# Packed products for four batches in two row tiles, and the first batch through DRAM, in an attention and mixture-of-experts kernel

## The chip, the core and the metric

The kernel runs as one program on one core of a Trainium2 chip. The metric is the device time of one execution in microseconds; the median of three runs of the kernel before is 1287.91 us (1282.92 to 1290.34). A core has TensorE (PE in the profile, its weight loads PEld), VectorE (DVE), ScalarE (ACT), GpSimd (POOL) and SyncE (SP). Each engine works through its own queue in order. Here SP issues nearly all DMAs.

## The reference, cut to what matters

```python
def sm_attn(qq, kk, vv):                       # softmax(scale * qq kk^T) vv
    ...
p_packed = sm_attn(p, k, v)                    # p: 8 batches, 8 heads, 32 rows of 64; k, v: 576 rows
x = sm_attn(q, p_packed, p_packed)             # q: 576 rows; every head attends to 32 packed rows
x = x.transpose(0, 2, 1, 3).reshape(4608, 512)
h = np.maximum(x @ w_in, 0.0)                  # w_in 512 x 2048
x2 = (h * h) @ w_out                           # w_out 2048 x 512
logits = x2 @ w_gate + modality_bias[modality_id]
e = np.argmax(logits, axis=1)                  # one of 8 experts for each token
out[token] = gate[token] * (np.maximum(x2 @ w1[e], 0.0) @ w2[e])
```

The weights w_in and w_out come as 64-bit floats.

## The kernel before

The program has an attention part, a layer part and an expert part. In the expert part, and in the layer part from its second unit on, nothing is changed by hand.

**The trick of the first layer.** `softmax(...) @ p_packed @ w_in` is computed as `softmax(...) @ (p_packed @ w_in)`. The inner product is small: each batch and head has 32 packed rows, and with w_in they give a 256 x 2048 matrix a batch, called pw. The first layer is then a product of the second softmax (256 wide) with pw. To keep precision, each factor stands as two tiles, a high half (rounded to float32r by an ACT copy) and a low half (the difference), and a product is three matmuls: high by low, high by high, low by high.

**Attention (lines 283 to 348, and the loop at 888).** The work is cut into 16 quads: a batch and four of its heads. `att1` is a generator of four steps: score products L297 (two column tiles of 64), then maximum, exp (L310) and a scaling of the whole 128x576 tile (L315), then five transposes (L320, L321) and their copies (L322, L323), then the value products L329 and L330 and the copies of the packed rows into `pp32` (L334) and into `pphl`, the two halves (L346 on ACT, L347 on POOL). The loop starts a quad in each round and takes one step of each quad that is under way, so a quad ends three rounds after it starts. A round also takes two conversions of w_in (`convert`, lines 198 to 216: ACT, four DVE operations, ACT, POOL), from 64 bits to the two halves in `wbt`.

**The packed product (`pw_unit`, lines 352 to 378).** `pphl` holds a pair of batches and a pair of heads as a block-diagonal 128x128 tile. A unit is one pair of heads and 512 of the 2048 columns; for each of the four pairs of batches it takes three matmuls L361 of 128x128 by 128x512, one PSUM bank and one copy out. Pairs 1 to 3 go to the DRAM tile `pw_d`. Of pair 0, batch 0's half is split at once into the two halves of its blocks (L376 on ACT, L377 on POOL), and batch 1's half goes to `pw_d`. A batch read back from `pw_d` (`load_pw`, two DMAs for 512 columns, into one of two buffers called raw) is split in 16 blocks by `split_pw` (L404 on ACT, L405 on POOL). The blocks live in a ring of 18, `head` (8) and `ring` (10).

**Layers (the loop at 959).** The 4608 tokens are 12 units of 384. For each unit and each of 16 blocks f, `layer1` multiplies (L473), ACT makes relu, square and high half (L482 to L484), the low half follows (L486: POOL in the first unit, DVE later), and `layer2` (L493) adds to three PSUM banks. `layer2` needs w_out in `wbt`, and w_out is converted into the very slots that w_in leaves: conversion u of w_out waits for all packed products of unit u. `others(u)`, called ahead of the first unit and in it, emits what is left of the packed products and one conversion of w_out.

**What sets the order.** The kernel is written in one order; a scheduler in the build then gives each engine its own, from a timeline that it works out itself. So a `yield` or a call count moves the emission, and only through the scheduler the place in a queue.

Of the kernel before, what the change touches and what calls it, by code (L numbers as in the profile page):

```python
# [26 lines left out]
def tile_pack_attention_moe_moe2(  # L27
# [33 lines left out]
    PAIRS = B // 2  # L61
    UPP = NUN // PAIRS
# [34 lines left out]
    pphl = pw_p.tile([P, PAIRS, 2, HP, 2 * P // 2], F32R, name="pphl")  # L97
# [42 lines left out]
    pw_d = tc.dram_tile([PAIRS, HP, P, DFF], F32, name="pw_d")  # L140
# [80 lines left out]
    PW = {9 + i: [(0, 2 * i), (0, 2 * i + 1)] for i in range(4)}  # L221
    PW |= {13 + i: [(1, 2 * i), (1, 2 * i + 1)] for i in range(6)}
    for i in range(3):
        PW[16 + i].append((2, i))
    A20 = 4
# [57 lines left out]
    def att1(i):  # L283
# [23 lines left out]
        sm = a_p.tile([P, 1], F32, tag="sm", name="sm")  # L307
# [7 lines left out]
        nc.scalar.activation(out=a, in_=a, func=AF.Copy, scale=sm)  # L315
# [8 lines left out]
        yield  # L324
        pq = bank("t", "pq")
        for g in range(2):
            ds, ns = slice(2 * g * D, 2 * (g + 1) * D), slice(2 * g * NPK, 2 * (g + 1) * NPK)
            for r in range(4):
                nc.tensor.matmul(pq[:, ns], vt[:, r, ds], aT[:, r, ns], start=(r == 0), stop=False)  # L329
            nc.tensor.matmul(pq[:, ns], vl[:, ds], aT[:LAST, 4, ns], start=False, stop=True)  # L330
        load_v(i + 4)
        gs = slice(2 * qd, 2 * qd + 2)
        for j in range(2):
            nc.vector.tensor_copy(  # L334
                pp32[j * D : (j + 1) * D, b, gs, j * NPK : (j + 1) * NPK],
                pq[j * D : (j + 1) * D, :P].rearrange("p (g i n) -> p g i n", g=2, i=2)[:, :, j, :],
            )
        hl = pphl[:, b // 2].rearrange("p x g (b n) -> p x g b n", b=2)
        if b < 2:
            places = [(slice(2 * qd + i, 2 * qd + i + 1), (b + i) % 2) for i in range(2)]  # L340
        else:
            places = [(gs, b % 2)]
        for g, o in places:
            src = pp32[:, b, g, :]
            hi = hl[:, 0, g, o, :]
            nc.scalar.activation(out=hi, in_=src, func=AF.Copy)  # L346
            nc.gpsimd.tensor_tensor(out=hl[:, 1, g, o, :], in0=src, in1=hi.bitcast(F32), op=ALU.subtract)  # L347
# [4 lines left out]
    def pw_unit(bp, u, so=None):  # L352
        if (bp, u) in made:
            return
        made.add((bp, u))
        fb, hp = divmod(u, HP)
        w = wbt[:, u]
        hl = pphl[:, bp]
        ph = bank("t", "pw")
        for i, (x, y) in enumerate(((0, 1), (0, 0), (1, 0))):  # L360
            nc.tensor.matmul(ph, hl[:, x, hp], w[:, y, :], start=(i == 0), stop=(i == 2))  # L361
        if so is None:
            so = pw_p.tile([P, 512], F32, tag="w5", name="pws", bufs=3)
        if bp % 2:
            nc.vector.tensor_copy(so, ph)
        else:
            nc.scalar.activation(out=so, in_=ph, func=AF.Copy)
        cs = slice(fb * 512, (fb + 1) * 512)
        if bp:
            nc.sync.dma_start(pw_d[bp, hp, :, cs], so)  # L370
        else:
            lo = slice((hp % 2) * 64, (hp % 2) * 64 + 64)
            up = slice(64 - (hp % 2) * 64, 128 - (hp % 2) * 64)
            t = blocks(4 * fb, 4)[lo, :, :, hp // 2, :]
            pv = so[lo].rearrange("p (k f) -> p k f", k=4)
            nc.scalar.activation(out=t[:, :, 0, :], in_=pv, func=AF.Copy)  # L376
# [511 lines left out]
    for i in range(len(quads) + 3):  # L888
# [5 lines left out]
        if i >= 3:  # L894
            runs.pop(0)
# [18 lines left out]
    def others(u):  # L914
        for v in range(min(u + HP + 1, NU)):
            pw_unit(0, v)
# [144 lines left out]
```

## Time and profile before

| | |
|---|---|
| median of three runs | 1287.91 us |
| profiled execution | 1283.14 us, span 1281.3 us |
| mean granted TensorE clock | 0.977 of full |
| PE busy | 1234.5 us (96%) |
| PE weight loads | 1029.2 us (80%) |
| DVE, ACT, POOL busy | 810.7, 600.7, 323.9 us |
| last score product L297 ends | 108.8 us |
| first layer-2 matmul L493 starts | 143.2 us |

A busy time is an interval that the engine's instructions cover. A matmul's interval begins where it enters the array and includes its way through, so those of neighbours overlap: the time that one costs in a stream is the distance between starts, not its own length. A float32 matmul shows as two, a float32r matmul as one. In a row, `128*64` is the part of the array that a matmul uses, rows by columns. What stands in brackets at a row's end is the idle time of the engine before it and what ended that.

### The profile page before, as it was taken

The page shows a single profiled execution, that of the slowest core. Times are in us where ns is not written, and L with a number is a line of the kernel's source. Part 1 is how long each engine was busy: PE and PEld are TensorE (multiplying, and loading weights), DVE is VectorE, ACT ScalarE, POOL GpSimd, SP SyncE. Part 2 cuts the span into 40 slices and gives each one's busy share as a digit, 9 for nine tenths or more (in the row PEclk, how much of TensorE's full clock was granted, in tenths as well). Part 3 has the DMA queues.
Part 4 walks back from the last instruction along what each step waited for, and adds up shares of the span by engine and source line. Part 5 has one row for each costly group of instructions (what it writes and reads, how often), then busy time and mean ns, then how long its engine had stood idle before and what let it go on. Part 6 is the DMA issues. An engine that isn't in the chain of part 4 may idle for free.

```text
span 1281.3 us, 18377 instructions
## 1 busy us (share of the span) xinstructions
PE 1234.5 (96%) x6356; PEld 1029.2 (80%) x6356; DVE 810.7 (63%) x2040; ACT 600.7 (47%) x1209; POOL 323.9 (25%) x389
## 2 busy tenths in 40 slices
PE   7789999999999999999999999999999999999995
PEld 5567778788888888888888888878888888888884
DVE  4886866759676875767597396977644354354331
ACT  3575465555545565545654555642332343243220
POOL 4653456323101232012320033100221132022011
PEclk8798999999999999999999999989999999999998
DMA  9886665521211312012120122241442452353210
GB/s 343 285 293 197 181 172 174 165 76 51 67 43 29 89 50 76 32 35 76 50 84 17 34 68 83 90 152 51 173 152 99 146 181 95 121 198 111 87 67 36
DMA packets 74167, 145.06 MB, mean 113 GB/s; under 512 B 6608, under 2 KB 26192, under 8 KB 73936
## 3 DMA queue, kind: packets, MB, share of 16 engines
q1 hardware_dynamic: 68304, 124.62, 30.2%
q0 software_dynamic: 5760, 19.17, 4.5%
q8 instruction: 52, 0.85, 0.3%
q14 instruction: 51, 0.42, 0.1%
HBM read 109.92 MB, written 33.85 MB: 112 GB/s over the span
## 4 chain that ended last, share of the span: by engine, by line
PE 86%; DVE 5%; DMA 5%; ACT 2%; issue 1%; POOL 1%; SPq 0%; POOLq 0%; ACTq 0%; DVEq 0%
PE acc L493 28%; PE ph L473 16%; PE h L780 15%; PE o L802 15%; PE s L428 2%; PE pq L329 2%; PE pw L361 2%; DMA wraw<-in_moe_w 1%; PE tr L760 1%; PE s L297 1%; DMA wgb<-in_moe_w_out 1%; DMA rows<-in_moe_w_out 1%; PE pq L330 1%; PE ta L455 1%; PE ta L320 1%
## 5 line engine op out<-in xcount | busy, mean ns | idle before, releaser
L493 PE MATMUL acc<-wbt,ghl 128*128 128x512 f32 x1728 | 443.8, 399 | 0.0
L493 PEld LDWEIGHTS acc<-wbt,ghl 128*128 128x128 f32 x1728 | 316.5, 189 | 61.1 <-ACT ghl L484 0.4
L514 DVE SCALAR_TENSOR_TENSOR rows<-rows,wgb 128x512 f32<-128x512 f32 x288 | 217.2, 754 | 3.9
L780 PE MATMUL h<-xt,wbt 128*128 128x512 f32 x864 | 214.9, 399 | 0.0
L780 PEld LDWEIGHTS h<-xt,wbt 128*128 128x128 f32 x864 | 163.1, 189 | 39.0
L486 DVE TENSOR_TENSOR ghl<-r,ghl 128x384 fp32r<-128x384 f32 x176 | 108.0, 615 | 113.2 <-ACT ghl L484 112.5
L473 PE MATMUL ph<-a2T,ring 128*128 128x384 f32 (+1 forms) x840 | 145.2, 309 | 2.6 <-ACT ring L404 2.6
L484 ACT ACTIVATE ghl<-r 128x384 fp32r<-128x384 f32 x192 | 100.2, 522 | 98.4 <-PE acc L493 96.7
L473 PEld LDWEIGHTS ph<-a2T,ring 128*128 128x128 f32 x840 | 129.8, 190 | 10.8 <-ACT ring L404 3.0
L482 ACT ACTIVATE r<-ph 128x384 f32<-128x384 f32 x192 | 92.9, 486 | 89.1 <-PE ph L473 83.0
L791 DVE SCALAR_TENSOR_TENSOR ht<-h,ht 128x512 fp32r<-128x512 f32 x72 | 49.2, 688 | 117.9 <-ACT ht L790 117.9
L813 POOL DMA_INDIRECT out<-wgb,idx_s x36 | 36.5, 1013 | 342.5 <-DVE wgb L811 251.4
L473 PE MATMUL ph<-a2T,head 128*128 128x384 f32 (+1 forms) x696 | 118.9, 308 | 0.3 <-ACT r L482 0.3
L802 PE MATMUL o<-head,ht 128*128 128x512 f32 x432 | 113.6, 398 | 3.4 <-ACT ht L790 3.2
L790 ACT ACTIVATE ht<-h 128x512 fp32r<-128x512 f32 x72 | 42.5, 593 | 149.9 <-PE h L780 149.8
L802 PE MATMUL o<-ring,ht 128*128 128x512 f32 x432 | 111.6, 394 | 0.0
L473 PEld LDWEIGHTS ph<-a2T,head 128*128 128x128 f32 x696 | 106.1, 190 | 6.6 <-ACT r L482 0.4
L483 ACT ACTIVATE r<-r 128x384 f32<-128x384 f32 x192 | 100.0, 522 | 4.2
L802 PEld LDWEIGHTS o<-head,ht 128*128 128x128 f32 x432 | 81.0, 190 | 22.4 <-ACT ht L790 3.6
L405 POOL TENSOR_TENSOR ring<-praw,ring 128x256 fp32r<-128x256 f32 x62 | 52.0, 840 | 169.5 <-ACT ring L404 124.2
L802 PEld LDWEIGHTS o<-ring,ht 128*128 128x128 f32 x432 | 80.4, 188 | 16.9
L717 DVE TENSOR_TENSOR wbt<-wraw,wbt 128x1024 fp32r<-128x1024 f32 x36 | 44.1, 1225 | 47.7 <-ACT wbt L716 47.6
(210 smaller groups left out, 1470.1 us busy)
## 6 DMA issues: line engine op xcount, KB each, us to landing
wraw<-in_moe_w SPq DMA_DIRECT2D x72, 512.0 KB, 3.8
praw<-pw_d SPq DMA_DIRECT2D x56, 256.0 KB, 4.0
pw_d<-pws SPq DMA_DIRECT2D x48, 256.0 KB, 3.2
x_d<-rows SPq DMA_DIRECT2D x12, 792.0 KB, 4.1
qT<-in_q SPq DMA_DIRECT2D x36, 256.0 KB, 3.8
early<-in_v SPq DMA_DIRECT2D x16, 512.0 KB, 6.3
rows<-in_k SPq DMA_DIRECT2D x10, 576.0 KB, 6.4
wgb<-in_moe_w_out SPq DMA_DIRECT2D x11, 512.0 KB, 4.5
```

Source lines behind the costliest of these rows:

```text
L405: nc.gpsimd.tensor_tensor(out=t[:, 1], in0=raw, in1=t[:, 0].bitcast(F32), op=ALU.subtract)
L473: nc.tensor.matmul(ph[:, off : off + n], t[:, x, c, :], a[:, y, c, off : off + n], start=(i == 0), stop=(i == 3 * NPC - 1),)
L482: nc.scalar.activation(out=r, in_=ph, func=AF.Relu)
L483: nc.scalar.activation(out=r, in_=r, func=AF.Square)
L484: nc.scalar.activation(out=hl[:, 0], in_=r, func=AF.Copy)
L486: eng.tensor_tensor(out=hl[:, 1], in0=r, in1=hl[:, 0].bitcast(F32), op=ALU.subtract)
L493: nc.tensor.matmul(acc[t], hl[:, x, t * P : (t + 1) * P], wbt[:, f, y, :], start=(f == 0 and x == 0 and y == 0), stop=(f == NF - 1 and x = ...
L514: nc.vector.scalar_tensor_tensor(out=junk, in0=row[:, t, :DM], scalar=1.0, in1=wgb[:, e], op0=ALU.mult, op1=ALU.mult, accum_out=one)
L717: nc.vector.tensor_tensor(out=t[:, 1, :], in0=raw, in1=t[:, 0, :].bitcast(F32), op=ALU.subtract)
L780: nc.tensor.matmul(ph, half1[:, g % 2, c, x, f * P : (f + 1) * P], xs[c][:, y, :], start=(i == 0), stop=(i == 3 * NDC - 1),)
L791: nc.vector.scalar_tensor_tensor(out=h[:, 1, :], in0=ph, scalar=0.0, in1=h[:, 0, :].bitcast(F32), op0=ALU.max, op1=ALU.subtract)
L802: nc.tensor.matmul(po, hs[f][:, x, t * P : (t + 1) * P], second(f)[:, y, :], start=(i == 0), stop=(i == 3 * NFE - 1),)
```

## The change

- **Quads of batches.** `pphl` is held by head with four batches side by side (4 x 32 columns), with no zero blocks. A unit (`pw_unit`) serves four batches: two heads lie in the two halves of the partitions, and each is a product of 64 rows by 128 columns with `tile_position` 0 or 64, three matmuls a head, into a PSUM bank of its own. One bank is copied out by ACT, the other by DVE, and one DMA of 512 KB writes both. There are 32 units of six matmuls, where there were 64 of three.
- **Batch 0 through DRAM.** L376 and L377 go. Batch 0 is loaded and split as the others are; `others` emits its loads and splits. A load is now four DMAs of 32 partitions.
- **Value products in column tiles.** Each head's product is a matmul of its own with 32 columns, in four column tiles (L327). It gives the rows with heads on the partitions; the softmax's scaling is now applied to this 128x64 tile on its copy out (L333), and two matmuls with the identity (L339) bring it into the old layout. `att1` has one step more. The low half of `pphl` moves from POOL to DVE (L351).
- **Rounds.** The loop takes one conversion of w_in a round, in 16 rounds; packed products of the first quad of batches begin in round 12; att2(0) in round 6.

```diff
-    pphl = pw_p.tile([P, PAIRS, 2, HP, 2 * P // 2], F32R, name="pphl")
+    pphl = pw_p.tile([P, QUADS, 2, HP, 4, NPK], F32R, name="pphl")
...
-    pw_d = tc.dram_tile([PAIRS, HP, P, DFF], F32, name="pw_d")
+    pw_d = tc.dram_tile([QUADS, HP, P, 2, DFF], F32, name="pw_d")
...
-    PW = {9 + i: [(0, 2 * i), (0, 2 * i + 1)] for i in range(4)}
-    PW |= {13 + i: [(1, 2 * i), (1, 2 * i + 1)] for i in range(6)}
...
+    PW = {12 + i: [(0, 2 * i), (0, 2 * i + 1)] for i in range(8)}
+    A20 = 6
...
-        nc.scalar.activation(out=a, in_=a, func=AF.Copy, scale=sm)
         yield
...
+        pv = bank("t", "pv")
+        for r in range(5):
+            k = P if r < 4 else LAST
+            for h in range(4):
+                ns = slice(h * NPK, (h + 1) * NPK)
+                nc.tensor.matmul(
+                    pv[ns, :D], aT[:k, r, ns], (vt[:, r] if r < 4 else vl)[:, h * D : (h + 1) * D],
+                    start=(r == 0), stop=(r == 4), tile_position=(0, h * NPK),
+                )
+        load_v(i + 4)
+        pvs = a_p.tile([P, D], F32, tag="pvs", name="pvs", bufs=2)
+        nc.scalar.activation(out=pvs, in_=pv[:, :D], func=AF.Copy, scale=sm)
+        yield
...
-        for g in range(2):
-            ds, ns = slice(2 * g * D, 2 * (g + 1) * D), slice(2 * g * NPK, 2 * (g + 1) * NPK)
-            for r in range(4):
-                nc.tensor.matmul(pq[:, ns], vt[:, r, ds], aT[:, r, ns], start=(r == 0), stop=False)
-            nc.tensor.matmul(pq[:, ns], vl[:, ds], aT[:LAST, 4, ns], start=False, stop=True)
...
+        heads = ident.rearrange("p (g i n) -> p i g n", g=2, i=2)
+        for j in range(2):
+            nc.tensor.matmul(
+                pq[j * D : (j + 1) * D, : 2 * NPK].rearrange("p (g n) -> p g n", g=2), pvs, heads[:, j],
+                start=True, stop=True,
+            )
...
+        hl = pphl[:, b // 4, :, gs, b % 4, :]
+        nc.scalar.activation(out=hl[:, 0], in_=src, func=AF.Copy)
+        nc.vector.tensor_tensor(out=hl[:, 1], in0=src, in1=hl[:, 0].bitcast(F32), op=ALU.subtract)
...
-        ph = bank("t", "pw")
+        ph = [bank("t", "pw") for _ in range(2)]
         for i, (x, y) in enumerate(((0, 1), (0, 0), (1, 0))):
-            nc.tensor.matmul(ph, hl[:, x, hp], w[:, y, :], start=(i == 0), stop=(i == 2))
...
+            for j in range(2):
+                js = slice(j * D, (j + 1) * D)
+                nc.tensor.matmul(
+                    ph[j],
+                    pphl[js, q, x, hp].rearrange("p b n -> p (b n)"),
+                    w[js, y, :],
+                    start=(i == 0),
+                    stop=(i == 2),
+                    tile_position=(j * D, 0),
+                )
+        so = pw_p.tile([P, 2, 512], F32, tag="w5", name="pws", bufs=2)
+        nc.scalar.activation(out=so[:, 0], in_=ph[0], func=AF.Copy)
+        nc.vector.tensor_copy(so[:, 1], ph[1])
+        nc.sync.dma_start(pw_d[q, hp, :, :, fb * 512 : (fb + 1) * 512], so)
...
+            for i in range(2):
+                o = (2 * j + i) * NPK
+                nc.sync.dma_start(raw[o : o + NPK], src[j, i, bs, :, fb * 512 : (fb + 1) * 512])
...
-        pull(cv, 2)
-        if i == 8:
+        pull(cv)
+        if i == NU:
...
-        for v in range(min(u + HP + 1, NU)):
-            pw_unit(0, v)
+        if u == 0 or u % 4 == 1 and u < NF - 4:
+            load_pw(0, (u + 3) // 4)
+        for f in (0, 1) if u == 0 else (u + 1,):
+            if f < NF:
+                split_pw(0, f)
         if u < NU:
             pw_unit(1, u)
-            if not {(2, u), (3, u)} & made:
-                both = w_p.tile([P, 2, 512], F32, tag="raw", name="pws2")
...
             pull(co)
```

Lines of the changed kernel differ a little: L295 is the score product, L317 and L318 the transposes, L366 the packed product, L375 and L376 its copies out, L377 its write, L397 a read back, L403 and L404 the two halves of a block, L472 and L492 the two layers, L481 to L483 and L485 what stands between them, L216 the high half of a conversion.

**ACT, from the end of attention to the first layer-1 result.** Here `pws` are the copies of packed products, `pphl` the high halves of the packed rows, `atbuf` transposed tiles, and `head` and `ring` with `praw` high halves of blocks that were read back. Before:

```order
L322 ACTIVATE atbuf<-ta 128x512
L346 ACTIVATE pphl<-pp_85 128x2x64
L202 ACTIVATE wgb<-wgb 128x512
L367 ACTIVATE pws<-pw 128x512
L322 ACTIVATE atbuf<-ta 128x512
L346 ACTIVATE pphl<-pp_85 128x2x64
L367 ACTIVATE pws<-pw 128x512 x2
L346 ACTIVATE pphl<-pp_85 128x2x64
L215 ACTIVATE wbt<-wgb 128x512 x2
L482 ACTIVATE r<-ph 128x384
L483 ACTIVATE r<-r 128x384
```

Now:

```order
L403 ACTIVATE head<-praw 128x256 x4
L375 ACTIVATE pws<-pw 128x512 x2
L333 ACTIVATE pvs<-pv,sm 128x64
L350 ACTIVATE pphl<-pq 128x2x32
L375 ACTIVATE pws<-pw 128x512 x2
L333 ACTIVATE pvs<-pv,sm 128x64
L403 ACTIVATE ring<-praw 128x256 x4
L350 ACTIVATE pphl<-pq 128x2x32
L375 ACTIVATE pws<-pw 128x512 x3
L216 ACTIVATE wbt<-wgb 128x512
L375 ACTIVATE pws<-pw 128x512
L403 ACTIVATE ring<-praw 128x256 x4
```

Sixteen high halves of batch 0's blocks now stand among the copies: the first four, two by two, right behind the eighth L375, then the three groups of four that are seen here, and behind the last of them the first L481. None stood in this stretch before. In POOL's queue, twelve low halves of these blocks stand ahead of the first low half of w_out, and six more ahead of the first L485.

**SP, the same stretch.** Reads of `pw_d` into `praw` wait for the writes of their columns, and for the buffer that they fill. Before:

```order
L370 DMA pw_d<-pws 128x512 x3
L234 DMA wgb<-in_moe_w_out 128x1024
L370 DMA pw_d<-pws 128x512 x14
L234 DMA wgb<-in_moe_w_out 128x1024
L370 DMA pw_d<-pws_1226 128x512 x2
```

Now:

```order
L377 DMA pw_d<-pws 256x1x512 x2
L397 DMA praw<-pw_d 32x2x512 x2
L377 DMA pw_d<-pws 256x1x512
L397 DMA praw<-pw_d 32x2x512 x2
L377 DMA pw_d<-pws 256x1x512
L397 DMA praw<-pw_d 32x2x512 x2
L377 DMA pw_d<-pws 256x1x512
L397 DMA praw<-pw_d 32x2x512 x2
```

Reads of a quarter, four DMAs, now stand between the writes of single units. The first read of any block stood far behind the last of these rows before.

**PE, in the first unit of the layer part, with buffer numbers.** Here each `pw_` number is one PSUM bank: before, a unit of one pair of batches; now, one row tile of a unit. Before:

```order
L493 MATMUL acc_1335<-wbt_109,ghl_1321 128x512
L473 MATMUL ph_1504<-a2T_344,head_612 128x384 x5
L361 MATMUL pw_1290<-wbt_109,pphl_87 128x512 x3
L473 MATMUL ph_1504<-a2T_344,head_612 128x384
L473 MATMUL ph_1556<-a2T_344,head_612 128x384
L361 MATMUL pw_1300<-wbt_109,pphl_87 128x512 x3
L493 MATMUL acc_1333<-wbt_109,ghl_1388 128x512 x2
```

Now:

```order
L472 MATMUL ph_1842<-a2T_453,head_1227 128x384 x3
L366 MATMUL pw_1658<-wbt_109,pphl_87 128x512 x3
L472 MATMUL ph_1842<-a2T_453,head_1227 128x384 x3
L472 MATMUL ph_1892<-a2T_453,head_1227 128x384
L366 MATMUL pw_1707<-wbt_109,pphl_87 128x512 x3
L472 MATMUL ph_1892<-a2T_453,head_1227 128x384 x3
L366 MATMUL pw_1708<-wbt_109,pphl_87 128x512 x3
```

The two banks of a unit, 1707 and 1708 here, are written in two runs of three, with other matmuls between them, where the kernel's text alternates between the two.

## Rows read from the trace of the kernel before

**Rows 1.** Stages: start:end, length, then PE, PEld, DVE, ACT, POOL busy; PEclk, DMA.

```profile
88.10:108.80 20.70, 15.15 (x70) 8.93 (x69) 14.94 (x29) 15.06 (x29) 12.36 (x10) 0.78 0.42 129
108.80:143.20 34.40, 33.66 (x200) 28.76 (x199) 21.09 (x43) 17.07 (x35) 10.73 (x12) 0.99 0.59 201
143.20:237.70 94.50, 86.59 (x427) 70.70 (x427) 63.46 (x92) 55.50 (x114) 51.89 (x44) 0.98 0.67 197
237.70:1281.30 1043.60, 1026.75 (x5266) 869.26 (x5265) 646.84 (x1719) 466.31 (x937) 199.36 (x245) 0.99 0.26 85
```

**Rows 2.** Timelines of ACT, POOL and DVE, 88 to 106 us: start, length, what.

```profile
93.01 1.92 ACT L376 ACTIVATE head<-pws 64x512 fp32r<-64x512 f32 x3
...
93.71 3.95 POOL L377 TENSOR_TENSOR head<-pws,head 64x512 fp32r<-64x512 f32 x3 [1.51 <-ACT head L376]
...
92.06 0.68 DVE L209 SCALAR_TENSOR_TENSOR wgb<-stage,wgb 128x512 int32<-128x512 int32 x1
...
101.08 1.64 DVE L209 SCALAR_TENSOR_TENSOR wgb<-wgb 128x512 int32<-128x512 int32 x1
102.83 1.57 DVE L212 SCALAR_TENSOR_TENSOR wgb<-wgb 128x512 f32<-128x512 f32 x1
```

**Rows 3.** PE's timeline, end of the stage ahead of layer 2.

```profile
139.01 2.26 PE L361 MATMUL pw<-wbt,pphl 128*128 128x512 f32 x9
141.11 2.25 PE L473 MATMUL ph<-a2T,head 128*128 128x384 f32 x12
143.20 1.55 PE L493 MATMUL acc<-wbt,ghl 128*128 128x512 f32 x6
```

**Rows 4.** PE's timeline, one quad's value products, and what follows them.

```profile
60.10 1.10 PE L329 MATMUL pq<-atbuf,early 128*128 128x64 f32 x8
...
62.90 0.55 PE L320 MATMUL ta<-ident,abuf 128*128 128x128 f32 x3
```

**Rows 5.** PE's timeline around matmuls in column tiles of 64.

```profile
360.10 0.69 PE L428 MATMUL s<-pp,qT 128*64 128x64 f32 x12
360.72 0.44 PE L473 MATMUL ph<-a2T,head 128*128 128x384 f32 x1
...
515.26 0.68 PE L428 MATMUL s<-pp,qT 128*64 128x64 f32 x8
515.87 1.31 PE L473 MATMUL ph<-a2T,ring 128*128 128x384 f32 x6
517.11 0.33 PE L428 MATMUL s<-pp,qT 128*64 128x64 f32 x2
517.37 1.20 PE L493 MATMUL acc<-wbt,ghl 128*128 128x512 f32 x4
```

**Rows 6.** Groups by line, 0 to 230 us: busy us, mean ns.

```profile
L367 ACT ACTIVATE pws<-pw 128x512 f32<-128x512 f32 x32 | 18.6, 586 | 10.4 <-PE pw L361 10.3
L315 ACT ACTIVATE abuf<-abuf,sm 128x576 f32<-128x576 f32 x16 | 12.2, 768 | 4.8 <-DVE sm L314 2.6 <-DVE mx L309 2.1
L484 ACT ACTIVATE ghl<-r 128x384 fp32r<-128x384 f32 x16 | 8.3, 519 | 2.4 <-PE acc L493 2.3
...
L405 POOL TENSOR_TENSOR ring<-praw,ring 128x256 fp32r<-128x256 f32 x1 | 0.7, 731 | 2.4 <-ACT ring L404 2.4
L404 ACT ACTIVATE ring<-praw 128x256 fp32r<-128x256 f32 x2 | 0.7, 408 | 3.0 <-DMA praw<-pw_d 3.0
```

**Rows 7.** Reads (L395) and writes (L370) of `pw_d`: issue ns min/median/max, then landing us.

```profile
L395 SPq DMA_DIRECT2D praw<-pw_d x56: 573/588/1227, 222.5 to 751.1; - x56
...
DMA to landing us min/median/max: 3.4/4.0/9.3
...
L370 SPq DMA_DIRECT2D pw_d<-pws x48: 319/320/544, 110.5 to 225.8; - x48
...
DMA to landing us min/median/max: 2.3/3.2/6.5
```

**Rows 8.** PE's timeline, batch 1's first block in the second unit.

```profile
229.42 1.17 PE L473 MATMUL ph<-a2T,ring 128*128 128x192 f32 x4 [2.60 <-ACT ring L404]
```

## What was predicted

> **What bounds the kernel now.** I read the table by stages first, then the chain of waits, then the timelines of PE, ACT, POOL and DVE in the stages that the change touches. The reader is to see in the table [rows 1] that from 237.7 us on PE is busy for 1026.75 of 1043.60 us: that part is bound by TensorE, and the order of the changed program is there the same as before, save for four DMAs a block load where there were two. So the question is the first 237.7 us. I cut them where the last score product L297 ends (108.8) and where the first layer-2 matmul L493 begins (143.2). Between the two PE is busy 33.66 of 34.40 us, and from 143.2 to 237.7 it is 86.59 of 94.50. Before that, from 88.1 to 108.8, it is busy 15.15 of 20.70 and nothing else is full either: that stage is a chain of short waits. In it [rows 2] ACT runs three L376 (1.92 us) and POOL three L377 (3.95 us), both making batch 0's blocks out of SBUF, ahead of the last w_in conversion, whose end DVE awaits; then DVE's next conversion runs at 1.64 us an operation beside three more L377, where the same operation took 0.68 a little earlier.
>
> **The change part by part, by stages.** The sum is made against the profiled execution: 1283.1 us, of which 1281.3 are the span.
>
> *To 88.1 us: 0.* The edit "one conversion per step" moves nothing here: the scheduler had put 10.8 conversions ahead of the tenth maximum and 17.8 ahead of the last, and now 10.8 and 17.5. The scaling of the whole 128x576 tile goes (16 of 768 ns on ACT [rows 6]) and 16 low halves come from POOL to DVE, at a quarter of L405's 731 ns [rows 6] for a quarter of its elements, 2.9 us in all. ACT isn't full there; DVE is nearer to it. I take 0, with -3 to +3.
>
> *88.1 to 108.8: -6.5.* Batch 0 no longer goes through L376 and L377. Without them POOL could begin the low half of the conversion at about 93.6 (93.01 and one activation of 0.59 [rows 2, 6]) where L377 held it to 97.66: 4.1 less; and three DVE operations lose 0.96 each, as the one shown, 2.9 less. I take 6.5 of these 7.0. From below, all from 93.0 to 104.4 could go (-12); from above nothing, if the loads of w_out, which now come next, hold DVE instead.
>
> *108.8 to 143.2, what PE must do: +0.9.* Counts are of this stage in the two orders. Five value products of 2.80 us each (60.10 to 62.90 [rows 4]) go: -14.0. Five of the new kind come, 40 halves each of 64 columns in four column tiles. No row shows those; the nearest is L428 in column tiles of 64: eight in one tile took 0.61 us (515.26 to 515.87), two took 0.26, so one more costs 0.058; but twelve over two tiles took 0.62 too [rows 5], so two tiles ran at once although the program gives all of one tile and then all of the other. Two at once for all makes 40 x 0.058 / 2 = 1.2 us, five times 6.0 (from 2.9, four at once, to 11.6, none). Five small products with the identity: 4 halves, two at once, 0.24 each, +1.2. Products with w_in: 54 matmuls of 0.233 (9 in 2.10 us, 139.01 to 141.11 [rows 3]) go, -12.6, and 90 come. Their order matters: the scheduler sets the three of one row tile before the three of the other, and often splits the two. Counting a run of L366 as long as the larger of its two halves, the 90 fill 60 slots, +14.0 (up to 21.0 with no overlap). Six layer-1 matmuls fewer at 0.174 (12 in 2.09 us [rows 3]): -1.0; four transposes fewer: -0.4. Changes of tile size: L428's two cost 0.14 beyond their own work, and L473's six between two such excursions took 1.24 where 6 x 0.174 is 1.04 [rows 3, 5]; 0.34 for two changes, 0.17 each. The stage has 50 now; of the 25 before, 20 are in the 2.80: +45 x 0.17 = 7.7. Sum: 34.4 - 14.0 + 6.0 + 1.2 + 1.4 - 1.0 - 0.4 + 7.7 = 35.3.
>
> By the Trainium skill (TensorE: Matmul & The Clock Gate, Part 3, the speedup against the span model) four column tiles cost little more than one, which is the 2.9 end for the value products and would take 3.1 us off the sum. The same part (what overlaps and what doesn't) calls matmuls strictly first in, first out; by that only the neighbours at a seam of two row tiles overlap, and I count 68 slots here and 5 more in the next stage, 3.0 us more. The row of twelve speaks against it [rows 5], as far as it goes.
>
> *The same stage, what ACT waits for: +18.1 more.* This is the term that decides. Batch 0's blocks now come back from DRAM: a write, four reads, then per block a high half on ACT (0.41) and a low half on POOL (0.73) [rows 6]. These high halves stand in ACT's queue in front of the copies that free PSUM for PE, four times. From the eighth w_in product's copy on, in ACT's order: write 0.32, two reads at 0.59 on SP, landing 4.0 [rows 7]: the first blocks at 5.5; four high halves with two copies at 0.59 and three short ones: 9.5. POOL ends its four low halves by 9.2, and only then may SP (the buffer) read the second quarter: reads and a write 2.8, landing 4.0, so 15.9; four halves and two copies: 18.7. The third quarter needs the write of the last of these (0.32 and landing 3.2 [rows 7]) and two reads: 27.4; then four halves, a short one and two copies: 30.5. The fourth, the same way, is on ACT at 39.1, and behind it the first ReLU chain, two more halves and the high half L484 (0.52): the first layer-2 matmul at 43. PE's own work reaches the eighth copy 10.4 us into the stage (two value products 2.4, 24 matmuls in 12 slots 2.8, small ones 1.8, 13 changes 2.2, one copy of a transposed tile and the copy itself). So the stage takes 53.4 instead of 34.4: +19.0, of which 0.9 is PE's. Bounds: +0.9, if landings are so quick that PE's work always covers them, to +40, if all four take the 9.3 of the slowest landing [rows 7]. I take +19.0, by the median landing.
>
> *143.2 to 237.7: -5.* 108 matmuls of the w_in product go here and 78 come, in 66 slots: -42 x 0.233 = -9.8. 44 more changes of tile size: +7.5. Batch 1's first load no longer comes late: the wait of 2.60 us at 229.42 [rows 8] goes. -4.9; from -12, if the other 5 us without PE go with it, to +5, if the conversions of w_out, behind twelve of POOL's low halves, are late next.
>
> Sum: 0 - 6.5 + 19.0 - 5 = +7.5, 1290.6 against the profiled execution. The four executions shown of before (with the profiled one) have a mean of 1286.1, 3.0 above it, and their median of three runs is 4.8 above it; I add 2.4: **1293 us**, +7.5 (0.6%) like for like. About 0.5%, 6.4 us, is what a measurement can tell from no change.
>
> **The rivals.**
> *A, the trips are covered.* The landings are done when ACT reaches the halves, since PE, with its tile changes, is later than I think. For it: PE's sum alone is 35.3 of the 53.4. Against: in the one place where the kernel before reads such a block just in time, ACT and PE waited [rows 8]. Then -6.5 + 0.9 - 5 = -10.6: 1275, faster. It decides as soon as a trip takes no longer than the 4 to 5 us of PE work between two of them.
> *B, the trips are longer.* Writes of 512 KB, w_out loads and reads share the queues; half way to the slowest landing adds 4 x 2.65 = 10.6: 1304, and all the way 1314. For it: 3.4 to 9.3 [rows 7]. Row tiles that don't overlap would come to the same side (30 + 12 slots, +9.8).
> *C, nothing to speak of.* The stage before 108.8 keeps its length, since the w_out conversions need their loads, and half of the trips' wait is covered: +6.5 less half of 18: about -1.5, 1284. The change then does in count what it says, and the time doesn't follow.
>
> **How the numbers follow.** Forecast 0.48 (its own range 1285 to 1302, like for like 0 to +16): slower 0.27, same 0.21. A 0.25: faster 0.21, same 0.04. B 0.15: slower. C 0.12: same 0.08, faster 0.04. Together faster 0.25, same 0.33, slower 0.42. The range reaches to A's and B's middle: 1272 to 1308.
>
> **What would show it.** The first layer-2 matmul at 150 to 160 us; ACT idle before L403 four times for 3 to 6 us each, released by a DMA of praw; PE idle before L339, L366 and L472 in the same places. L377's and the 1.64 us operations gone, the last L295 done by about 102. L327 about 1.2 us a step; L366 in pairs 7 to 40 ns apart inside a run. No wait before batch 1's first L472. It is wrong in its main term if ACT waits less than 8 us in all for praw before the first layer-2 matmul, and wrong in its confinement if the time from the second unit on differs by more than 2 us.

## The result and the profile after

The changed kernel takes 1304.41 us (median of four, 1302.08 to 1304.53), the kernel before beside it 1287.72. The ratio is 1.0135, with a 95% interval of 1.0111 to 1.0159: slower by 1.35%, where 0.6% was forecast. The profiled execution has a span of 1302.7 us, 21.4 more than the profiled one of before, which was one of the faster executions of its kernel.

The stages of the kernel after, cut where the fourteenth quad's score products begin, where the last ones end, at the first layer-2 matmul, and at the 145th (where [rows 1] ends the first unit); columns as there:

```profile
0.00:96.30 96.30, 70.39 (x646) 37.69 (x646) 68.51 (x171) 40.29 (x92) 38.19 (x65) 0.72 0.87 302
96.30:111.90 15.60, 9.99 (x86) 5.27 (x85) 10.75 (x27) 6.54 (x15) 3.17 (x3) 0.72 0.52 174
111.90:175.00 63.10, 47.00 (x347) 30.14 (x347) 22.31 (x52) 24.72 (x61) 12.98 (x18) 0.69 0.61 201
175.00:256.90 81.90, 81.26 (x382) 59.04 (x382) 57.97 (x85) 48.19 (x99) 42.89 (x38) 0.98 0.56 196
256.90:1302.70 1045.80, 1029.35 (x5288) 871.33 (x5286) 646.11 (x1722) 469.07 (x941) 199.12 (x246) 0.99 0.27 85
```

Against [rows 1] the first cut comes 8.2 us late, the next stage is 5.1 shorter, the third 28.7 longer, the fourth 12.6 shorter. The rest is 2.2 longer by this cut, but from the 301st layer-2 matmul on (297.9 us before, 319.4 after) the difference stays at 21.4 to 21.5: the loss is where the change is. In the third stage TensorE idles for 16.1 us, where it idled for 0.7, and it is busy for 47.0 us, where it was for 33.66, although it was given less to do. The granted clock is 0.69 where it was 0.99. The clock's records say the same: ahead of 245 us TensorE was at the lower level (1.2 GHz) for 105.8 us, before for 41.0. At full clock 47.00 us at 0.69 would be some 32 us (an estimate from the row).

What ACT waited for in that stage, batch 0's high halves on ACT's timeline:

```profile
133.22 0.72 ACT L403 ACTIVATE head<-praw 128x256 fp32r<-128x256 f32 x2 [7.05 <-DMA praw<-pw_d]
134.33 0.71 ACT L403 ACTIVATE head<-praw 128x256 fp32r<-128x256 f32 x2
142.88 1.33 ACT L403 ACTIVATE head<-praw 128x256 fp32r<-128x256 f32 x4 [4.34 <-DMA praw<-pw_d]
156.13 1.33 ACT L403 ACTIVATE ring<-praw 128x256 fp32r<-128x256 f32 x4
171.16 1.33 ACT L403 ACTIVATE ring<-praw 128x256 fp32r<-128x256 f32 x4 [5.14 <-DMA praw<-pw_d]
```

These are the forecast's trips: four, three of them waited for, 16.5 us in all. But PE's timeline in the same stage shows something else as well:

```profile
146.73 0.42 PE L327 MATMUL pv<-early,atbuf 128*32 128x64 f32 x2
147.08 0.79 PE L366 MATMUL pw<-wbt,pphl 64*128 64x512 f32 x1
147.80 0.42 PE L327 MATMUL pv<-early,atbuf 128*32 128x64 f32 x2
148.16 0.48 PE L339 MATMUL pq<-ident,pvs 128*64 128x64 f32 x2
```

No wait stands here, and yet one packed product with two value products takes 1.08 us (147.08 to 148.16): other work is mixed in singly, at the lower clock.

### The profile page after: what moved, and what is told of

Read it like the earlier page. It is cut to its first block, busy times and chain, and to the rows that moved or that the text cites. A ratio compares the mean times of both kernels' runs of the same rounds, so it can differ in the third digit from the quotient of the medians.

```text
span 1302.7 us, 19209 instructions
## 1 busy us (share of the span) xinstructions
PE 1238.0 (95%) x6740; PEld 1003.5 (77%) x6740; DVE 805.7 (62%) x2056; ACT 588.8 (45%) x1205; POOL 296.4 (23%) x369
## 4 chain that ended last, share of the span: by engine, by line
PE 85%; DVE 6%; DMA 5%; ACT 2%; issue 1%; POOL 1%; SPq 0%; POOLq 0%; ACTq 0%; DVEq 0%
PE acc L492 29%; PE ph L472 16%; PE h L779 15%; PE o L801 15%; PE s L427 2%; PE pw L366 2%; PE s L295 2%; DMA wraw<-in_moe_w 1%; PE tr L759 1%; DMA praw<-pw_d 1%; PE ta L317 1%; DMA pw_d<-pws 1%; PE pv L327 1%; PE ta L454 1%; DVE wgb L207 0%
## 5 line engine op out<-in xcount | busy, mean ns | idle before, releaser
L492 PE MATMUL acc<-wbt,ghl 128*128 128x512 f32 x1728 | 444.4, 400 | 0.0
L492 PEld LDWEIGHTS acc<-wbt,ghl 128*128 128x128 f32 x1728 | 315.5, 189 | 64.1 <-issue 4.4
L485 DVE TENSOR_TENSOR ghl<-r,ghl 128x384 fp32r<-128x384 f32 x176 | 108.3, 616 | 121.9 <-ACT ghl L483 118.2
L472 PE MATMUL ph<-a2T,ring 128*128 128x384 f32 (+1 forms) x840 | 144.4, 309 | 0.0
L483 ACT ACTIVATE ghl<-r 128x384 fp32r<-128x384 f32 x192 | 100.3, 522 | 95.9 <-PE acc L492 93.0
L481 ACT ACTIVATE r<-ph 128x384 f32<-128x384 f32 x192 | 93.1, 485 | 93.6 <-PE ph L472 88.8
L472 PEld LDWEIGHTS ph<-a2T,ring 128*128 128x128 f32 x840 | 128.7, 190 | 8.4 <-issue 1.1
L472 PE MATMUL ph<-a2T,head 128*128 128x384 f32 (+1 forms) x696 | 121.7, 311 | 5.1 <-ACT r L481 5.1
L472 PEld LDWEIGHTS ph<-a2T,head 128*128 128x128 f32 x696 | 107.9, 192 | 12.7 <-ACT r L481 5.6
L404 POOL TENSOR_TENSOR ring<-praw,ring 128x256 fp32r<-128x256 f32 x70 | 57.6, 828 | 177.0 <-ACT ring L403 124.7
L404 POOL TENSOR_TENSOR head<-praw,head 128x256 fp32r<-128x256 f32 x58 | 47.9, 831 | 151.5 <-ACT head L403 135.5
```

The source lines that it names most:

```text
L404: nc.gpsimd.tensor_tensor(out=t[:, 1], in0=raw, in1=t[:, 0].bitcast(F32), op=ALU.subtract)
L472: nc.tensor.matmul(ph[:, off : off + n], t[:, x, c, :], a[:, y, c, off : off + n], start=(i == 0), stop=(i == 3 * NPC - 1),)
L481: nc.scalar.activation(out=r, in_=ph, func=AF.Relu)
L483: nc.scalar.activation(out=hl[:, 0], in_=r, func=AF.Copy)
L485: eng.tensor_tensor(out=hl[:, 1], in0=r, in1=hl[:, 0].bitcast(F32), op=ALU.subtract)
L492: nc.tensor.matmul(acc[t], hl[:, x, t * P : (t + 1) * P], wbt[:, f, y, :], start=(f == 0 and x == 0 and y == 0), stop=(f == NF - 1 and x = ...
```

## The experiments

The theories have letters in the expectations: W (waits on the trips, and the clock as their consequence), C (half-array matmuls by themselves hold the clock down), then D and R, M and G, and H, as each text says. The ratios are to the kernel before on the same chip, with 95% intervals.

**A bare run of the new shapes** (`micro`): `full` is a 128x128 by 128x512 matmul; a loop of row-tiled ones as below (abridged).

```diff
+ for u in range(40):                       # six of a unit: 000111; then the same with i and j exchanged
+     for j in range(2):
+         for i in range(3):
+             matmul(bank[j], x[64*j:64*j+64, :P], x[64*j:64*j+64, 512:], tile_position=(64*j, 0))
```

> Leaves out the whole computation: TensorE alone runs, without a pause, full matmuls (128x128 by 128x512), then 40 units of six row-tiled ones in the order 000111, full ones, the same in the order 010101, full ones, 12 sets of 40 value products in four column tiles, full ones, 30 rounds of three full ones and one row-tiled pair, full ones. Theory W (the time went into waits on the DRAM trips, and the low granted clock of the tail is their consequence): the granted clock stays at 1.0 through all sections once it has risen; a unit of 000111 takes between 0.7 us (the two tiles run at once) and 1.3 us (first in, first out, a seam overlapped). Theory C (half-array matmuls by themselves hold the clock down): the clock falls to 0.5 in the sections of row tiles or column tiles, though the engine never waits, and rises in the full ones; a unit of row tiles takes twice what W says.

PE's timeline, the two orders and the full ones between and after; then the alternation:

```profile
29.08 27.52 PE L62 MATMUL bank<-x 64*128 64x512 f32 x240
56.53 13.92 PE L55 MATMUL bank<-x 128*128 128x512 f32 x60
70.38 27.52 PE L68 MATMUL bank<-x 64*128 64x512 f32 x240
...
139.86 0.50 PE L81 MATMUL bank<-x 64*128 64x512 f32 x2
140.29 0.97 PE L78 MATMUL bank<-x 128*128 128x512 f32 x3
141.19 0.50 PE L81 MATMUL bank<-x 64*128 64x512 f32 x2
```

A unit takes 0.69 us in either order, at a clock of 1.0: two row tiles run at once even if the program gives three of the one and then three of the other. C falls in its plain form; only right behind the column-tiled section, whose 480 matmuls had three pauses of 1.05 to 1.74 us, do the records fall, for 3.4 us. A round of three full ones and a pair takes 1.33 us (139.86 to 141.19), where four slots of 0.232 are 0.93: 0.2 us for each of its two changes of tile size.

**Batch 0's high halves late** (`late`): they are queued on ACT behind the last copy of the first units, later ones behind the layers.

```diff
-                split_pw(0, f)
+                with tc.issue_after(held["behind"]):   # the last ACT copy of a unit, later the last L483
+                    split_pw(0, f)
```

> As the changed kernel, but batch 0's high halves stand in ACT's queue behind the last copy of the first four batches' products, and those of later blocks behind the first layers. Theory W: the 16.5 us that ACT waits for batch 0's reads before the first layer-2 matmul go, TensorE's 16 us of idle with them, and with the gaps the half clock: 1276 to 1288 us, first layer-2 matmul at 142 to 158 us, mean granted clock of the 45 us before it above 0.9. Theory C: the waits go, but the row-tiled and column-tiled work still runs at half clock: 1292 to 1302 us, clock below 0.75 there.

1298.67 us, 1.0099 [1.0070, 1.0128]. In the profiled execution, the shortest of its ten (1291.89 us), ACT waits for no read of batch 0 any more, and the first layer-2 matmul comes at 160.0 instead of 175.0. PE's busy time in the stage ahead of it:

```profile
110.70:160.00 49.30, 44.09 (x346) 29.42 (x347) 22.56 (x51) 23.44 (x53) 8.86 (x10) 0.73 0.69 227
```

The idle time falls from 16.1 to 5.2 us, and the clock stays at 0.73. So W falls where it said that the clock would follow; the number lies in C's range. The trips are worth some 0.4%, about 5 us, and the two intervals overlap.

**Pairs of batches, batch 0 through DRAM** (`pairs_dram`): the kernel before, without L376 and L377; `others` loads and splits batch 0 as in the changed kernel, and emits batch 0's products two units sooner.

```diff
-            nc.scalar.activation(out=t[:, :, 0, :], in_=pv, func=AF.Copy)
-            nc.gpsimd.tensor_tensor(...)
-            nc.sync.dma_start(pw_d[0, hp, 64:128, cs], so[up])
+        nc.sync.dma_start(pw_d[bp, hp, :, cs], so)
```

> As the kernel before (pairs of batches, full 128-row products, value products as they were), only batch 0 goes through DRAM like the others, loaded and split as in the changed kernel. Theory W: the trips alone cost the loss: 1298 to 1308 us, ACT idle before the high halves of batch 0 for 10 to 20 us in all. Theory C: no half-array products, so the clock stays up and most of the loss is absent: 1285 to 1294 us.

1289.70 us, 1.0025 [0.9996, 1.0054]. Its stages from 88.1 us, cut as above:

```profile
88.10:103.20 15.10, 13.05 (x69) 8.64 (x68) 9.45 (x25) 9.29 (x20) 3.87 (x4) 0.89 0.56 179
103.20:142.70 39.50, 37.34 (x202) 31.64 (x202) 23.92 (x47) 21.45 (x47) 13.38 (x18) 0.91 0.70 227
```

The stage that L376 and L377 held up is 5.6 us shorter than in [rows 1], as forecast, and the next one 5.1 longer; ACT waits for batch 0's reads 2.8 us ahead of the first layers and 10.0 us in all to 240, as W said, but the time that W put on it isn't there. The move through DRAM, the 5.6 us that it saves included, costs about 0.25%, in C's range, and the interval holds no change at all.

**Value products in column tiles alone** (`col_only`): the kernel before with the new L327 and L339.

```diff
-                nc.tensor.matmul(pq[:, ns], vt[:, r, ds], aT[:, r, ns], ...)
...
+                    pv[ns, :D], aT[:k, r, ns], (vt[:, r] if r < 4 else vl)[:, h * D : (h + 1) * D], ...
```

> As the kernel before, only the value products go in column tiles of 32 with the small product with the identity, one step more in each quad; products by pairs, batch 0 straight from SBUF. Theory W: less TensorE work and no new wait: 1278 to 1287 us. Theory C: the clock falls in the attention part, 1288 to 1298 us, granted clock before 108 us lower than in the kernel before (0.81 and 0.88 there).

1290.83 us, 1.0033 [1.0003, 1.0063]: less work for TensorE and no gain, in C's range and outside W's. Between the fourteenth quad's scores and the end of the last ones:

```profile
92.80:114.90 22.10, 16.14 (x126) 8.12 (x125) 16.56 (x26) 13.63 (x27) 15.18 (x12) 0.52 0.33 92
```

The clock is 0.52 here, 0.78 in the same stage before. So C's times came out in all three kernels, though its plain mechanism fell in the bare run; TensorE also waits in this stage, for 6.0 us.

**The old value products in the new frame** (`late_oldvp`, `after_oldvp`), with the high halves late and where the change has them; and the first with the six of a unit alternating (`late_oldvp_alt`). A quad has one step less, so the units start a round earlier.

```diff
-        pvs = a_p.tile([P, D], F32, tag="pvs", name="pvs", bufs=2)
...
+        nc.scalar.activation(out=a, in_=a, func=AF.Copy, scale=sm)
...
+                nc.tensor.matmul(pq[:, ns], vt[:, r, ds], aT[:, r, ns], start=(r == 0), stop=False)
```

> The packed products by head in row tiles and batch 0 through DRAM with its high halves late, as in the experiment before, but the value products as in the kernel before (128 rows by two heads, no column tiles, no product with the identity, one step less). Theory D (the column-tiled value products, with their extra step and their changes of tile size, keep the engine at 1.2 GHz): the clock recovers, above 0.9 in the 45 us before the first layer-2 matmul, and the halved packed products show: 1268 to 1282 us. Theory R (it is the row-tiled products among other work that do it): clock below 0.8 there, 1290 to 1300 us.

> The changed kernel with the value products alone put back to those of the kernel before; batch 0's high halves stand where the changed kernel has them. Theory D: about half of the loss goes, 1285 to 1295 us, the waits of ACT for batch 0's reads (16.5 us before the first layer-2 matmul) stay. Theory R: 1299 to 1306 us. Theory W (waits alone): 1298 to 1304 us.

> As the first of this call, with the six products of a unit in the order 010101. In the bare run either order took 0.69 us a unit. Where the six stay together nothing changes; in the first unit's layers, where the scheduler puts other work between the three of one tile and the three of the other, the pairs overlap now: 16 units less 0.35 us, 5.6 us faster than the order 000111, if the pairs stay side by side; within 2 us of it, if they are parted as well.

1309.98 us, 1.0151 [1.0099, 1.0204]; 1314.80, 1.0196 [1.0153, 1.0239]; 1310.82, 1.0165 [1.0117, 1.0213]. The first two are slower than anything expected: D falls, and R's numbers are passed. The third lies within 2 us of the first, as its text has it for pairs that are parted as well. The first one's stage ahead of layer 2, in an execution of 1315.74 us, the longest of its four, and a stretch of it without a wait:

```profile
123.10:186.20 63.10, 59.57 (x223) 47.23 (x222) 21.68 (x53) 23.21 (x53) 8.08 (x10) 0.52 0.48 169
136.10:174.80 38.70, 38.70 (x146) 31.22 (x146) 10.34 (x29) 9.57 (x23) 0.00 (x0) 0.50 0.41 144
```

TensorE waits for 3.5 us here and is busy for 59.6, at half clock. In this trace the clock's records are at the lower level without a break from 114.9 to 183.2 us. No wait explains that length: the engine is slow, not held up. It isn't short waits that keep the clock down either, since in the second row TensorE works for all of 38.7 us. The four executions take the longer the lower their mean granted clock (1301.34 us at 0.954, 1315.74 at 0.936); the ten of `late` show no such order (1291.89 at 0.959, 1303.83 at 0.967). The order of the six changed nothing that these intervals can tell.

**Work kept together** (`late_contig`): the run with the high halves late, and, from the first unit on, each set of value products and each unit of packed products of the first four batches in one piece.

```diff
+        with in_turn(q == 0):          # queue on PE behind the last matmul of the set or unit before
             for i, (x, y) in enumerate(((0, 1), (0, 0), (1, 0))):
```

> As the run with batch 0's high halves late, and besides each set of 40 column-tiled value products and each unit of six row-tiled products stays together on TensorE from the first unit on (in the run with them late, from 138 to 147 us, one row-tiled product alternates with two value products). If the changes of tile size are what costs, by 0.2 us each: some 20 fewer, 4 us, and the clock a little higher: 1289 to 1295 us. If the shape of the column-tiled products costs: no change, 1296 to 1301 us.

1287.36 us, 0.9997 [0.9977, 1.0018]: the loss is gone. In PE's order of that stage stand 31 changes of tile size, where the change and the run `late` have 50 and the kernel before 26. Its row:

```profile
111.70:157.60 45.90, 37.14 (x349) 25.88 (x348) 21.93 (x51) 23.15 (x52) 7.96 (x9) 0.72 0.75 245
```

PE is busy for 6.95 us less than in `late`, 0.37 for each of the 19 changes that went, at a clock of 0.72. It waits for some 3.5 us more, so the stage is 3.4 shorter. The medians lie 11.3 us apart and the two profiled executions 4.3, that of `late` being its shortest: these traces don't show the whole gain.

What it costs to part a unit stands in the trace of the changed kernel, in the first unit's layers, at a clock of 1.0:

```profile
179.03 0.97 PE L366 MATMUL pw<-wbt,pphl 64*128 64x512 f32 x3
179.93 1.19 PE L492 MATMUL acc<-wbt,ghl 128*128 128x512 f32 x4
181.05 0.96 PE L366 MATMUL pw<-wbt,pphl 64*128 64x512 f32 x6
181.95 2.13 PE L492 MATMUL acc<-wbt,ghl 128*128 128x512 f32 x8
```

From start to start three matmuls of one row tile take 0.90 us, and six of both tiles 0.90 as well: half a unit by itself costs as much as a whole one, so a unit that is parted takes some 0.9 us more, its further change of tile size included.

**A bare run of whole steps** (`micro2`) and **useless work** (`late_oldvp_fill`).

```diff
+        for i in range(3 if q == 0 else 0):     # overwritten by the unit that follows
+            nc.tensor.matmul(ph[0], pphl[:, q, 0, hp]..., w[:, 0, :], start=i == 0, stop=i == 2)
```

> Leaves out the whole computation: TensorE alone, without a pause; between runs of 90 full matmuls (128x128 by 128x512) stand four sections of eight steps. Each step has the value products of a quad, four transposes and packed products: old value products with nine full packed products (the steps of the kernel before); old value products with two units of six row-tiled ones; column-tiled value products with two units of six row-tiled ones (the steps of the changed kernel, without the small product with the identity); column-tiled value products with nine full ones. Theory M (the low clock comes from the mix: short matmuls with few long full ones between them): the granted clock falls to 0.5 in the second section, and perhaps the third, though nothing is waited for, and stays at 1.0 in the first. Theory G (the low clock comes from the gaps and waits in the kernel alone): 1.0 in all four.

> As the run with the old value products and batch 0's high halves late (1310 us, where the clock was at 0.5 from 125.8 to 194.1 us), with three useless full 128-row products ahead of each of the first 16 units, into the bank that the unit then overwrites: 48 more matmuls of 0.233, 11.2 us of work at full clock. Theory M: the added work brings the clock up in that stretch, and the kernel is not slower, 1285 to 1308 us. Theory G: the clock stays down and the time grows by the work, 22 us at half clock, 11 at full: 1318 to 1334 us.

(The times of the clock's records in this text, and the 22.6 us in the last expectation below, were read from another zero; on the trace's own scale they are 11 us less, so that the first rise took some 6 us, not 17.) In the bare run the clock stays at 1.0 in all four sections, of 23 to 42 us each: each of these mixes, unbroken, keeps a raised clock, so M is wrong as it stood. One step of the kernel before, and one of the changed kernel without its product with the identity, each to the start of the next, on PE's timeline:

```profile
28.82 2.76 PE L63 MATMUL bank<-raw 128*128 128x64 f32 x20
31.50 0.66 PE L73 MATMUL bank<-ident,raw 128*128 128x128 f32 x4
31.92 2.32 PE L83 MATMUL bank<-x 128*128 128x512 f32 x9
34.08 2.76 PE L63 MATMUL bank<-raw 128*128 128x64 f32 x20
...
151.59 0.77 PE L69 MATMUL bank<-raw 128*32 128x64 f32 x40
152.29 0.66 PE L73 MATMUL bank<-ident,raw 128*128 128x128 f32 x4
152.88 1.67 PE L79 MATMUL bank<-x 64*128 64x512 f32 x12
154.47 0.77 PE L69 MATMUL bank<-raw 128*32 128x64 f32 x40
```

5.26 us against 2.88: fed without a pause, with the pieces kept together and at full clock, the change nearly halves such a step. Yet the kernel with 48 useless matmuls more takes 1293.41 us, 1.0068 [1.0042, 1.0095], 0.8% less than without them by the two ratios, whose intervals don't meet. Its stage, at nearly full clock and with 1.7 us of waits:

```profile
115.40:163.20 47.80, 46.14 (x263) 33.68 (x264) 20.42 (x52) 24.66 (x57) 7.93 (x10) 0.96 0.71 242
```

G's numbers are far off, so neither theory holds as written. The useless matmuls also moved the scheduler's order (most units now stand in one piece), so not all of the 0.8% need be the clock's.

**A bare run with pauses** (`micro3`): sections of several mixes, each after a pause.

```diff
+    def rest():
+        for i in range(12):
+            nc.scalar.activation(out=x, in_=raw, func=AF.Copy)   # TensorE waits for x
+        pair(bank[0])
```

> Leaves out the whole computation: TensorE alone, 90 full matmuls, then six sections, each after a pause of some 12 us (while ACT rewrites an operand) and three full matmuls: 16 steps of old value products, transposes and two row-tiled units; 16 steps of old value products, transposes and nine full packed products; 20 steps of column-tiled value products, transposes and two row-tiled units; the same with three full matmuls more in each; 20 times four row-tiled units alone; 90 full matmuls. Theory H (a mix with few full matmuls keeps a raised clock, as the second bare run showed, but does not raise a fallen one): the clock is 0.5 after each pause; it rises in the second and fourth sections and in the full ones, and in the first it stays at 0.5 to the end, some 140 us; in the third it stays down or rises late. Theory G (only pauses lower the clock, and any work without pause raises it alike): it rises after about the same time in every section, 17 us or less, as it did in the full matmuls at the start of the bare runs (5.6 to 22.6 us).

Each pause of 13.2 us brought the clock down. From the restart to the return of the higher level, with the stretch after the first rise as the second row; then the other five sections in the order of the text:

```profile
41.00:60.30 19.30, 19.30 (x76) 15.37 (x77) 0.00 (x0) 0.00 (x0) 0.00 (x0) 0.50 0.00 0
60.30:129.00 68.70, 68.70 (x498) 55.86 (x500) 0.00 (x0) 0.00 (x0) 0.00 (x0) 1.00 0.00 1
143.10:152.50 9.40, 9.40 (x33) 8.15 (x34) 0.00 (x0) 0.00 (x0) 0.00 (x0) 0.50 0.00 0
245.60:251.50 5.90, 5.88 (x57) 4.26 (x59) 0.00 (x0) 0.00 (x0) 0.00 (x0) 0.50 0.01 3
320.00:323.10 3.10, 3.10 (x45) 2.18 (x46) 0.00 (x0) 0.00 (x0) 0.00 (x0) 0.50 0.00 0
406.80:411.90 5.10, 5.10 (x19) 3.67 (x21) 0.00 (x0) 0.00 (x0) 0.00 (x0) 0.50 0.00 0
477.90:483.60 5.70, 5.69 (x13) 4.46 (x14) 0.00 (x0) 0.00 (x0) 0.00 (x0) 0.50 0.00 0
```

Every mix comes back here, but not alike, with one restart of each: old value products with row-tiled products worked for 19.3 us at half clock, with full packed products for 9.4, the changed kernel's mix for 5.9, with three full ones more for 3.1. The 9.4 and the 19.3 stand apart; whether 3.1 and 5.9 differ by more than chance was not tried. H is right that the mix decides, wrong that the first one never rises and the third only late. But in `late_oldvp` the kernel's own mix of old value products, transposes and row-tiled products, fed without a break for 38.7 us, did not come back at all, twice as long as the first one here needed. What the bare mix lacks of it is not known.

**A version that beats both** (`best`): work kept together, high halves late, the six alternating, and three buffers for the copies.

```diff
-        so = pw_p.tile([P, 2, 512], F32, tag="w5", name="pws", bufs=2)
+        so = pw_p.tile([P, 2, 512], F32, tag="w5", name="pws", bufs=3)
...
+                    tc.add_manual_dep(mm.ins, last.ins.name, NOSYNC, reason="alternate")
```

> The changed kernel with batch 0's high halves late, each set of column-tiled value products and each unit of packed products kept together (1287.4 us so far), and besides three buffers for the copies of packed products where two made ACT and DVE wait 14.6 and 16.3 us for their writes in the stretch from 100 to 160 us, and the six of a unit in the order 010101, so that they overlap in the first unit's layers. If the changes of tile size and the buffers are what is left: 5 to 10 us off, 1277 to 1283 us, faster than the kernel before by 0.3 to 0.7%. If the clock decides alone: within 3 us of 1287.

1279.18 us (median of ten), 0.9958 [0.9945, 0.9971]: faster than the kernel before by 0.4%, and 1.8% below the changed one by the two ratios. Its stage ahead of layer 2, and a wait on PE that is left in it:

```profile
113.40:152.10 38.70, 29.33 (x290) 20.49 (x290) 18.37 (x42) 19.68 (x46) 7.65 (x10) 0.76 0.76 249
```
```profile
129.93 0.42 PE L322 MATMUL tb<-ident,abuf 128*64 128x128 f32 x1 [6.20 <-ACT pws L387]
```

The waits of the copies for their writes (14.6 us on ACT and 16.3 on DVE in `late_contig`, 100 to 160 us) are no longer among the larger ones. In the wait shown, ACT's copy stands behind a w_out conversion (L204) that waited 6.17 us for its load. Which share of the last 0.4% is the buffers' and which the alternation's was not tried apart.

## Why the prediction was right or wrong

- **Direction and place: right.** Slower, in the first 240 us, and the expert part the same; behind the first unit 2.2 us came on top, where the text's own sign allowed 2. Two edits take the loss away: the high halves late (1.0135 to 1.0099) and the work kept together (to 0.9997).
- **The time: in the stated range, by the rivals' reach.** The forecast's own range ended at 1302, and two of its signs failed: the first layer-2 matmul came at 175.0 (150 to 160 was said), the last score product at 111.9 (about 102).
- **88.1 to 108.8, -6.5: right.** -5.1 here, -5.6 in `pairs_dram`.
- **ACT's waits for the trips: right as a wait, wrong as a price.** 16.5 us of waits against 18.1 in the sum, four visits, the reads' median landing 4.1 us (2.5 to 5.1). But taking them away gives only some 5 us: 1.0135 to 1.0099, and with the old value products 1.0196 to 1.0151. When ACT no longer waits for reads, its copies wait for the two buffers (7.1 us in `late`) and for a slow TensorE (10.4). Rival B's time, 1304, came out, not its mechanism, so that is luck: landings were no longer than the median assumed.
- **TensorE's work, +0.9 in the third stage: the step that failed.** It priced every matmul with durations of stretches at a clock of 0.99 to 1.00. At full clock its sum was not too low: 47.0 us at 0.69 are some 32 there, where it has 35.3. The value products were too dear (40 with their change take 0.7 in the bare run, not 1.2). The count of slots was sound: a unit takes 0.69 us, three slots, only in one piece, and the scheduler parted many, 18 runs of three against 4 of six in the first unit's layers. What it left out is the clock: 47.0 us busy, at 0.69. Long waits alone don't explain that: `late` took 11 us of them away and has 0.73, and in the changed kernel TensorE is busy for all of the 8.20 us from 88.1 to 96.3, at 0.50. That the low clock is dear, and that full matmuls in the mix hold it up, is what the useless matmuls point to: 0.96 for 0.52, and 0.8% won, in the frame of `late_oldvp`.
- **A change of tile size at 0.17: too small.** The count was right (50 against 25, by the trace 26), the bare price 0.2 at full clock. In the kernel, keeping the work together took 0.37 of busy time for each change that went, and 1.0% of the time. Part of that is row tiles that now meet their partners (three alone take 0.90 us, six in one piece too); how much, the runs don't tell.
- **Strictly first in, first out:** so the Trainium skill (TensorE: Matmul & The Clock Gate, Part 3) has matmuls start and end. If then only neighbours at a seam overlap, an unbroken stream of units of 000111 takes four slots a unit, 0.93 us (an estimate at 0.232 a slot). The bare run doesn't bear it out: 0.69 was measured. In the kernel the overlap isn't always whole: in `late_contig` two units in one piece take 2.06 us (113.90 to 115.96, at 1.0), where six slots and a change are 1.6.
- **To 88.1 us, 0: wrong.** The fourteenth quad's scores come 8.2 us later. Of this 4.7 come with the column tiles alone (92.8 in `col_only`); from 59.0 to there the clock is 0.69 after, and 1.00 before from 59.0 to 88.1.
- **First unit's layers, -5:** -12.6, or -10.4 when the 2.2 behind it are counted, near the lower bound of -12. The wait of [rows 8] went, as forecast; TensorE is busy for 81.26 of 81.90 us.
- **Rival C's sum: wrong by its own terms.** With +6.5 for the stage that keeps its length and half of the wait gone, +7.5 + 6.5 - 9 is +5, not -1.5.

What stays open: what kept the clock of `late_oldvp` down for 68 us. Its waits (0.7 to 1.9 us) did not, as far as the 38.7 us without one tell, and a bare mix of the same kinds came back after 19.3. Why the clock falls in the changed kernel is open with it.

## What to carry to other kernels

A matmul made cheaper can cost time where TensorE is fed by other engines: here waits, parted row tiles, changes of tile size and a lower clock outweighed what was saved. Price the work after a change at both levels of the clock, and look in the stage's row for the granted clock before taking a duration from it. Keep matmuls of one tile size, and row tiles that should run at once, together in the engine's order; what a scheduler mixes, a dependency without a wait can part.

## What the runs showed of the hardware

Two row tiles run at once though the queue holds three of one and then three of the other (27.52 us for 240, the same as alternating); three of one alone take 0.90 us, and so do six of both. A pause of 13 us was followed by 3.1 to 19.3 us at the lower clock level, by the kind of work, and in a kernel 38.7 us of work without a pause did not end it (0.50). And 48 useless matmuls made a kernel 0.8% faster, its clock 0.96 for 0.52 in the stage.
